# Two low-part products of 64 rows, each on its half of the array, in an fp32r SwiGLU kernel

## The chip, the cores and the metric

The kernel runs on one core of one Trainium2 chip. The metric is device time in microseconds, from runs of the whole program. Before the change the median of three runs is 514.69 us (514.53 to 514.96).

## The reference

The reference is one block of a network on 2048 tokens of 448 channels: an adaptive layer norm, a state-space convolution, a second adaptive layer norm and a SwiGLU feed-forward part with 1792 hidden units. Everything is in 32-bit floats. Cut to what matters:

```python
h = _layernorm(x, axis=-1) * (1 + ca) + sa
x = x + ga * _A_ref(h, ...)                      # the convolution
h = _layernorm(x, axis=-1) * (1 + cb) + sb
g = _silu(h @ w_gate)                            # 448 -> 1792
u = h @ w_up                                     # 448 -> 1792
x = x + gb * ((g * u) @ w_down)                  # 1792 -> 448
```

## The kernel before

The tokens are cut into 16 tiles of 128 and the tiles into six blocks of 2, 2, 3, 3, 3 and 3 tiles (`BLOCKS`). For each block `ffn` loops over the 14 slices of 128 hidden units (`f`). I call one pass of this loop a step. Each step does `gate_up(f)` and then `down(f - 1)`; between the two, and after them, small pieces of the work for the next block are put in from a table written by hand (`TIMES`, `todo`).

**Splitting into parts.** TensorE multiplies numbers of type float32r, so each operand is split into a high part (the cast to float32r) and a low part (what the cast left over). A product is the sum of high x high, low weight x high, and high weight x low. The activations lie transposed, channels on the partitions, in `hhi` and `hlo`: `[128, 4, tokens]`, four groups `k` of 128 channels. There are only 448 channels, so the fourth group has 64. These last 64 channels are laid down twice, on partitions 0 to 63 and again on 64 to 127 (`make_xn`, L162, writes channels 384 to 447 a second time).

**The weights.** `wgu[j]` is `[128, 2, 7, 128]` for slice `j`: index 0 of the second axis is gate, 1 is up. Slots 0 to 2 are the high parts of the first three groups, slots 3 to 5 their low parts. Slot 6 holds the last 64 channels in both parts: the high part on partitions 0 to 63, the low part on 64 to 127. One product of slot 6 with `hhi` thus gives high x high and low weight x high at once. `split_w` (L84 to L95) makes these parts: ScalarE casts into slots 0 to 2 and into all of slot 6, VectorE subtracts into slots 3 to 5 (L93) and into the lower half of slot 6 (L95). It runs in the prologue for slices 0 and 1 and in block 0 for the others, two steps ahead of their use.

**The products of a step.** `gate_up` takes two PSUM banks, `ps[0]` for gate and `ps[1]` for up. For each, `mm(s, False)` multiplies by `hhi`: seven products (two for each of three groups, one for slot 6). `mm(s, True)` multiplies by `hlo`: four products (slots 0, 1, 2 and 6). So there are 11 products for gate and 11 for up, 22 in a step, all of 128 rows and 128 columns of weights, with 384 columns of activations (256 in the blocks of two tiles). The order is gate high, gate low, up high, up low. In the very first step (`head`) it is gate high, up high, gate low, up low.

**After them.** ScalarE takes Silu of gate's bank (L657), VectorE multiplies it with up's bank (L662), ScalarE casts the result to its high part (L665) and VectorE makes its low part (L666). `down(f - 1)` (L677) then multiplies the previous step's result by the down weights, three products of 448 columns for each tile, into the banks `dn`, which collect over all steps. At the end of a block the next block's activations are transposed on TensorE (L169) and split.

**The prologue.** Before the first block TensorE computes modulation rows and the state of the convolution. Some of these products use weights with few columns: L186 with one column, L212 (`mod_col`) with 128 columns and then twice 64, L419 with 33. L389 are full products just ahead of L186. L231 are products that only keep TensorE running.

The queues of each engine run in the order in which the program issues the instructions. No DMA and no GpSimd work is touched by the change.

Of the kernel before, what the change touches and what calls it, by code (L numbers as in the profile page):

```python
# [12 lines left out]
OP = mybir.AluOpType  # L13
# [25 lines left out]
def f32(ap):  # L39
    return ap.bitcast(F32)  # L40
# [3 lines left out]
def tile_kernel(ctx, tc, x, a_re, a_im, b_re, b_im, c_re, c_im, log_dt, dskip,  # L44
                wg, wu, wd, c, w_mod, dft, idft, out):
    nc = tc.nc
    sy, ve, sc, po, pe = nc.sync, nc.vector, nc.scalar, nc.gpsimd, nc.tensor
# [7 lines left out]
    def bank():  # L55
        t = psg.tile([128, 512], F32, name="bank")
        return t
# [5 lines left out]
    def load_x(i):  # L63
        if i < NT:
            xs[i] = xbuf[i % len(xbuf)]
            sy.dma_start(xs[i], x[i * 128:(i + 1) * 128, :])
# [19 lines left out]
    def split_w(j, part=None):  # L86
        hi, lo, st = wgu[j][:, :, 0:3, :], wgu[j][:, :, 3:6, :], wgu[j][:, :, 6, :]
        w = raw[j]
        if not part:
            sc.copy(hi, w[:, :, 0:3, :])  # L90
            sc.copy(st, w[:, :, 3, :])
        if part is None or part == 1:
            ve.tensor_tensor(lo, w[:, :, 0:3, :], f32(hi), op=OP.subtract)  # L93
        if part is None or part == 2:
            ve.tensor_tensor(st[64:128], w[64:128, :, 3, :], f32(st[64:128]), op=OP.subtract)  # L95

    ident = const.tile([128, 128], F32)
    tri = const.tile([128, 128], F32R)
# [8 lines left out]
    hlo = const.tile([128, 4, MB * 128], F32R)  # L107
# [50 lines left out]
    def make_xn(i, new, src=None):  # L158
        src = xs[i] if src is None else src
        xn[i] = new()  # L160
        for o, a, n in ((0, 0, D), (D, 384, 64)):
            ve.tensor_scalar(xn[i][:, o:o + n], src[:, a:a + n], *n2.of[i], op0=OP.subtract, op1=OP.mult)  # L162
# [74 lines left out]
    with tc.tile_pool(name="pre", bufs=1) as pre, tc.tile_pool(name="wm", bufs=6) as wm:  # L237
# [146 lines left out]
        for q in range(2):  # L384
            ve.tensor_tensor(v1[q], h01[q], gm1, op=OP.mult)
        mm = [(0, ident, hd[0]), (0, tri, vh[0]), (1, all1, vh[0]), (1, ident, hd[1]), (1, tri, vh[1]), (1, tri, vl[1]),
              (0, tri, vl[0]), (1, all1, vl[0]), (0, ramp, v1[0]), (1, far, v1[0]), (1, ramp, v1[1])]
        for z, (q, u, v) in enumerate(mm):
            pe.matmul(os[q], u, v, start=False, stop=z in (8, 10))  # L389
        split_w(0, 0)  # L390
        scaled(wms[3], (0, 1, 2, 3))
        sb_ = added(wms[3])
# [20 lines left out]
        for z in (1, 2):  # L413
            split_w(0, z)
        transposes(TILES[0])
        o = psd.tile([128, 512], F32, name="cv")[:, 0:D]
        mm = [(left[:, 0], v) for v in vh + vl] + [(left[:, 1 + q], v1[q]) for q in range(2)]
# [200 lines left out]
    def run_blocks(pools, st, first=None):  # L618
        work, hid = pools.work, pools.hid
        new_xn = lambda: work.tile([128, 512], F32, name="xn", bufs=MB)  # L620
        def ffn(ts, fresh, last, todo):
            n = len(ts) * 128
            dn = [psd.tile([128, 512], F32, name=f"dn{q}") for q in range(len(ts))]
            pp, wp = {}, {}
            qz = [(q, z) for z in range(3) for q in range(len(ts))]

            def split_d(j):
                if last:
                    po.tensor_tensor(wdn[j], wdn[j], gb, op=OP.mult)
                hi = hid.tile([128, D], F32R, name="wdh")  # L630
                lo = hid.tile([128, D], F32R, name="wdl")
                sc.copy(hi, wdn[j])  # L632
                po.tensor_tensor(lo, wdn[j], f32(hi), op=OP.subtract)  # L633
                wp[j] = hi, lo

            def gate_up(f, nw):
                head = fresh and f == 0
                if not head:
                    split_d(f)
                w = wgu[f]  # L640
                p = hid.tile([128, MB * 128], F32, name="p")
                hi = hid.tile([128, MB * 128], F32R, name="phi")
                lo = hid.tile([128, MB * 128], F32R, name="plo")
                ps = [psd.tile([128, 512], F32, name="dn2") if head else bank(), bank()]

                def mm(s, lo):

                    parts = ((0,), (1,), (2,), (6,)) if lo else ((0, 3), (1, 4), (2, 5), (6,))
                    for k, ws in enumerate(parts):
                        for a in ws:  # L650
                            pe.matmul(ps[s][:, 0:n], w[:, s, a], (hlo if lo else hhi)[:, k, 0:n],  # L651
                                      start=not lo and a == 0, stop=lo and k == 3)

                for s, z in ((0, False), (1, False), (0, True), (1, True)) if head else (
                        (0, False), (0, True), (1, False), (1, True)):
                    mm(s, z)
                sc.activation(p[:, 0:n], ps[0][:, 0:n], AF.Silu)  # L657
                if head:
                    split_d(f)
                elif nw is not None:  # L660
                    split_w(nw, 0)
                ve.tensor_tensor(ps[1][:, 0:n], p[:, 0:n], ps[1][:, 0:n], op=OP.mult)  # L662
                if nw is not None and not head:
                    split_w(nw, 1)
                sc.copy(hi[:, 0:n], ps[1][:, 0:n])  # L665
                ve.tensor_tensor(lo[:, 0:n], ps[1][:, 0:n], f32(hi[:, 0:n]), op=OP.subtract)  # L666
                if nw is not None:
                    split_w(nw, None if head else 2)
                pp[f] = hi, lo

            def down(f, qz):
                hi, lo = pp[f]
                wh, wl = wp[f]
                for q, z in qz:
                    cs = slice(q * 128, (q + 1) * 128)
                    u, v = ((hi, wh), (hi, wl), (lo, wh))[z]
                    pe.matmul(dn[q][:, 0:D], u[:, cs], v, start=f == 0 and z == 0, stop=f == NF - 1 and z == 2)  # L677

            for f in range(NF):
                more = fresh and f + 2 < NF  # L680
                gate_up(f, f + 2 if more else None)
                if more:
                    pools.load(f + 2 + NS)
                for g, a in todo.get((f, 0), []):
                    g(*a)
                if f and not (last and f == NF - 1):
                    down(f - 1, qz)
                for g, a in todo.get((f, 1), []):
                    g(*a)
            if last:  # L690
                down(NF - 2, qz[:-1])
                down(NF - 1, [(0, 0), (0, 1)])
                down(NF - 2, qz[-1:])
                down(NF - 1, [(0, 2)] + [(q, z) for q in range(1, len(ts)) for z in range(3)])
            else:
                down(NF - 1, qz)
            for q, i in enumerate(ts):
                t = dn[q][:, 0:D]
                if not last:
                    t = new_xn()[:, 0:D]  # L700
                    ve.tensor_tensor(t, dn[q][:, 0:D], gb, op=OP.mult)
                ve.tensor_tensor(xs[i], xs[i], t, op=OP.add)
                sy.dma_start(out[i * 128:(i + 1) * 128, :], xs[i])

        for j in range(NP0, NS + 2):
            pools.load(j)
        if first is not None:
            for i in TILES[1]:
                load_x(i)
            for i in TILES[0]:  # L710
                first(i)
                n2.stat(i, TILES[0])
            n2.root(TILES[0])
            for i in TILES[0]:
                make_xn(i, new_xn)
            transposes(TILES[0])
        for b, ts in enumerate(TILES):
            todo = {}
            if b + 1 < len(TILES):
                nx = TILES[b + 1]  # L720

                def at(f, late, g, *a):
                    todo.setdefault((f, late), []).append((g, a))

                if b:
                    for i in nx:
                        at(0, 1, load_x, i)
                root1, *times, root2, shift = TIMES[min(b, 2)]

                def go(h, g, *a):  # L730
                    at(h // 2, h % 2, g, *a)

                for q, (i, hs) in enumerate(zip(nx, times)):
                    at(1 if b else q, 1, n1.stat, i, nx)
                    for h, g in zip(hs, st):
                        go(h, g, i)
                    go(h, n2.stat, i, nx)
                go(root1, n1.root, nx)
                go(root2, n2.root, nx)
                for h, i in zip(shift, nx):  # L740
                    go(h, make_xn, i, new_xn)
                at(NF - 1, 0, transposes, nx)
                if b == 0:
                    at(2, 1, end_gate)
            ffn(ts, b == 0, b + 1 == len(TILES), todo)
# [137 lines left out]
```

## Time and profile before

| | us |
|---|---|
| median of three runs | 514.69 |
| the profiled execution | 511.07 |
| its span, first to last instruction | 509.3 |
| TensorE products busy | 484.7 |
| TensorE weight loads busy | 453.9 |
| VectorE busy | 290.7 |
| GpSimd busy | 225.2 |
| ScalarE busy | 187.5 |

A row of a timeline gives the start, the length, the engine, the line of the kernel, the operation, what is written and read, the shapes and the count. PE is TensorE's products and PEld its loads of weights. For a product, `128*33` is rows x columns of the weights and `128x448` is partitions x columns of the moving operand. Products overlap: each is shown from its start to its modelled end, after the next one has begun, so the time that a product takes in a stream is read from the distance of the starts and not from the length. A row of the windows gives a stretch, its length, and then the busy time of each engine asked for with the number of instructions, and at the end the granted clock of TensorE, the share of the DMA engines and GB/s.

### The profile page before, as it was taken

Reading aid. Unit: us, or ns where it says so; the run is one execution under the profiler, and the core shown is the slowest. Engines: PE = TensorE matmul, PEld = TensorE weight load, DVE = VectorE, ACT = ScalarE, POOL = GpSimd, SP = SyncE. Lnnn points to the kernel's source line nnn. Section 1 sums busy time; section 2 is a strip of 40 time slices with the busy share of each in tenths; the row PEclk is TensorE's granted clock in tenths of the full one; section 3 lists DMA queues with packets and bytes.
Section 4 is the critical chain, followed back from the end, with each engine's and each line's share of the span. In section 5 each row is a group of like instructions: output and inputs, shape, how many; then the busy total and the mean of one; then the engine's idle time right before and its main releaser. Section 6 shows DMA issues by size and latency. Waiting matters only on the chain.

```text
span 509.3 us, 7301 instructions
## 1 busy us (share of the span) xinstructions
PE 484.7 (95%) x2747; PEld 453.9 (89%) x2747; DVE 290.7 (57%) x509; ACT 187.5 (37%) x388; POOL 225.2 (44%) x209
## 2 busy tenths in 40 slices
PE   7959988989999999999999999999999999999995
PEld 5536978879989999999899999989999989999995
DVE  2798899985786834763563575274366457211222
ACT  4347753743334422332422333243233234222221
POOL 1577474443785235553114474112556223344330
PEclk9958999999999999999999999999999999999999
DMA  7985555502000100000030000002000001000001
GB/s 220 298 204 164 169 159 145 145 1 91 1 1 2 61 31 1 0 2 0 1 108 1 2 0 2 0 36 74 1 0 2 0 1 55 0 1 1 1 0 62
DMA packets 25860, 26.07 MB, mean 51 GB/s; under 512 B 2232, under 2 KB 25144, under 8 KB 25816
## 3 DMA queue, kind: packets, MB, share of 16 engines
q1 hardware_dynamic: 25816, 25.52, 17.0%
q8 instruction: 23, 0.38, 0.3%
q14 instruction: 21, 0.17, 0.1%
HBM read 21.80 MB, written 3.67 MB: 50 GB/s over the span
## 4 chain that ended last, share of the span: by engine, by line
PE 79%; DVE 10%; issue 3%; ACT 2%; SPq 2%; DMA 2%; POOL 1%; DVEq 0%; ACTq 0%; POOLq 0%
PE bank L651 48%; PE dn L677 24%; DVE xn L162 2%; PE bank L186 2%; PE dn L389 1%; DMA dsk<-in_A_Dskip_dram 1%; DVE scr L333 1%; DVE plo L666 1%; DVE h L151 1%; PE bank L169 1%; PE bank L219 1%; DVE bank L662 1%; ACT phi L665 1%; SPq L84 1%; DMA raw<-in_B_w_up_dram 1%
## 5 line engine op out<-in xcount | busy, mean ns | idle before, releaser
L651 PE MATMUL bank<-hhi,gu 128*128 128x384 f32 (+1 forms) x1169 | 211.3, 320 | 0.0
L651 PEld LDWEIGHTS bank<-hhi,gu 128*128 128x128 f32 x1169 | 191.2, 188 | 2.7 <-issue 0.4
L633 POOL TENSOR_TENSOR wdl<-wd,wdh 128x448 fp32r<-128x448 f32 x84 | 102.2, 1218 | 201.2 <-ACT wdh L632 193.3
L651 PE MATMUL bank<-hlo,gu 128*128 128x384 f32 (+1 forms) x668 | 131.9, 319 | 0.0
L662 DVE TENSOR_TENSOR bank<-p,bank 128x384 f32<-128x384 f32 (+1 forms) x84 | 43.2, 514 | 140.0 <-PE bank L651 136.1
L651 PEld LDWEIGHTS bank<-hlo,gu 128*128 128x128 f32 x668 | 110.2, 188 | 0.0
L665 ACT CAST phi<-bank 128x384 fp32r<-128x384 f32 (+1 forms) x84 | 37.3, 444 | 147.7 <-DVE bank L662 147.7
L657 ACT ACTIVATE p<-bank 128x384 f32<-128x384 f32 (+1 forms) x83 | 37.9, 457 | 75.4 <-PE bank L651 75.3
L666 DVE TENSOR_TENSOR plo<-bank,phi 128x384 fp32r<-128x384 f32 (+1 forms) x84 | 43.0, 511 | 38.1 <-ACT phi L665 38.0
L677 PE MATMUL dn<-wdh,phi 128*128 128x448 f32 x224 | 60.1, 368 | 2.1 <-ACT phi L665 2.1
L677 PE MATMUL dn<-wdl,phi 128*128 128x448 f32 x224 | 59.6, 366 | 0.9 <-POOL wdl L633 0.9
L677 PE MATMUL dn<-wdh,plo 128*128 128x448 f32 x224 | 59.7, 367 | 0.6 <-DVE plo L666 0.6
L632 ACT CAST wdh<-wd 128x448 fp32r<-128x448 f32 x84 | 47.8, 569 | 33.3 <-PE dn L677 33.1
L677 PEld LDWEIGHTS dn<-wdl,phi 128*128 128x128 f32 x224 | 42.0, 188 | 4.7 <-POOL wdl L633 1.3
L677 PEld LDWEIGHTS dn<-wdh,plo 128*128 128x128 f32 x224 | 41.9, 188 | 4.6 <-DVE plo L666 1.2
L677 PEld LDWEIGHTS dn<-wdh,phi 128*128 128x128 f32 x224 | 39.7, 188 | 4.0 <-ACT phi L665 2.7
L762 POOL TENSOR_TENSOR v<-h,gm 128x448 f32<-128x448 f32 x14 | 16.1, 1153 | 14.0 <-DVE h L153 14.0
L769 POOL TENSOR_TENSOR v<-v,run 1x448 fp32r<-1x448 f32 x14 | 17.5, 1251 | 1.9 <-DMA run<-run 1.0
L778 POOL TENSOR_TENSOR h<-h,gd 128x448 f32<-128x448 f32 x14 | 17.6, 1258 | 0.0
L763 POOL TENSOR_TENSOR v<-h,g 128x448 fp32r<-128x448 f32 x14 | 17.6, 1254 | 0.0
L93 DVE TENSOR_TENSOR gu<-raw,gu 128x768 fp32r<-128x768 f32 x14 | 16.9, 1207 | 1.0 <-ACT gu L90 0.9
L772 ACT CAST vh<-v 128x448 fp32r<-128x448 f32 x14 | 7.9, 566 | 24.8 <-DVE v L768 24.8
(164 smaller groups left out, 434.3 us busy)
## 6 DMA issues: line engine op xcount, KB each, us to landing
wmt<-in_w_mod_dram SPq DMA_DIRECT2D x6, 784.0 KB
x<-in_A_u_dram SPq DMA_DIRECT2D x16, 224.0 KB
out_dram<-x SPq DMA_DIRECT2D x16, 224.0 KB
wd<-in_B_w_down_dram SPq DMA_DIRECT2D x14, 224.0 KB
raw<-in_B_w_gate_dram SPq DMA_DIRECT2D x14, 192.0 KB
raw<-in_B_w_up_dram SPq DMA_DIRECT2D x14, 192.0 KB
raw<-in_B_w_gate_dram SPq DMA_DIRECT2D x14, 64.0 KB
raw<-in_B_w_up_dram SPq DMA_DIRECT2D x14, 64.0 KB
```

The lines of the kernel that those rows point to most:

```text
L93: ve.tensor_tensor(lo, w[:, :, 0:3, :], f32(hi), op=OP.subtract)
L632: sc.copy(hi, wdn[j])
L633: po.tensor_tensor(lo, wdn[j], f32(hi), op=OP.subtract)
L651: pe.matmul(ps[s][:, 0:n], w[:, s, a], (hlo if lo else hhi)[:, k, 0:n], start=not lo and a == 0, stop=lo and k == 3)
L657: sc.activation(p[:, 0:n], ps[0][:, 0:n], AF.Silu)
L662: ve.tensor_tensor(ps[1][:, 0:n], p[:, 0:n], ps[1][:, 0:n], op=OP.mult)
L665: sc.copy(hi[:, 0:n], ps[1][:, 0:n])
L666: ve.tensor_tensor(lo[:, 0:n], ps[1][:, 0:n], f32(hi[:, 0:n]), op=OP.subtract)
L677: pe.matmul(dn[q][:, 0:D], u[:, cs], v, start=f == 0 and z == 0, stop=f == NF - 1 and z == 2)
L763: po.tensor_tensor(v1, h, gm1, op=OP.mult)
L769: po.tensor_tensor(v1[0:1], f32(v1[0:1]), run[0:1, 1, :], op=OP.add)
L778: po.tensor_tensor(h, h, gd, op=OP.mult)
```

## The change

The products of slot 6 with `hlo` change. Before, each was a product of 128 rows, in which the lower 64 rows multiplied the low weight with the low activation. After, each is a product of the 64 rows that hold the high weight. To let gate and up use different rows, up's slot 6 is laid out the other way round: its high part on partitions 64 to 127 and its low part on 0 to 63. The products of slot 6 with `hhi` are as before, since `hhi` holds the last 64 channels in both halves.

`split_w` makes the low part of slot 6 with two subtractions, each on 64 partitions and 128 columns, in place of one on 64 partitions and 256 columns.

In `gate_up`, `mm(s, True)` has three products, and a new function `both` issues the two products of 64 rows, one behind the other: gate's on rows 0 to 63 into `ps[0]`, up's on rows 64 to 127 into `ps[1]`. In all steps but the first, `both` stands between gate and up: its first product ends gate's sum, its second begins up's, and up's seven high products and three low ones follow. In the first step it stands between gate's low products and up's. A step still has 22 products.

The product of low weight with low activation of the last 64 channels, which the products of 128 rows had in addition, is no longer computed; for the other channels it never was.

```diff
         if part is None or part == 2:
-            ve.tensor_tensor(st[64:128], w[64:128, :, 3, :], f32(st[64:128]), op=OP.subtract)
+            for s, e in enumerate((slice(64, 128), slice(0, 64))):
+                ve.tensor_tensor(st[e, s], w[e, s, 3, :], f32(st[e, s]), op=OP.subtract)
...
                 def mm(s, lo):
-
-                    parts = ((0,), (1,), (2,), (6,)) if lo else ((0, 3), (1, 4), (2, 5), (6,))
+                    parts = ((0,), (1,), (2,)) if lo else ((0, 3), (1, 4), (2, 5), (6,))
                     for k, ws in enumerate(parts):
                         for a in ws:
                             pe.matmul(ps[s][:, 0:n], w[:, s, a], (hlo if lo else hhi)[:, k, 0:n],
-                                      start=not lo and a == 0, stop=lo and k == 3)
-
-                for s, z in ((0, False), (1, False), (0, True), (1, True)) if head else (
-                        (0, False), (0, True), (1, False), (1, True)):
-                    mm(s, z)
+                                      start=(s == 0 or head) and not lo and a == 0, stop=s == 1 and lo and k == 2)
+
+                def both(first):
+                    for s, e in enumerate((slice(0, 64), slice(64, 128))):
+                        pe.matmul(ps[s][:, 0:n], w[e, s, 6], hlo[e, 3, 0:n], start=s == 1 and first, stop=s == 0)
+
+                if head:
+                    mm(0, False)
+                    mm(1, False)
+                    mm(0, True)
+                    both(False)
+                    mm(1, True)
+                else:
+                    mm(0, False)
+                    mm(0, True)
+                    both(True)
+                    mm(1, False)
+                    mm(1, True)
```

## The prediction

> **What bounds the kernel now.** I read the page first: the busy shares, the granted clock, then the chain that ended last.
>
> ```profile
> span 509.3 us, 7301 instructions
> PE 484.7 (95%) x2747; PEld 453.9 (89%) x2747; DVE 290.7 (57%) x509; ACT 187.5 (37%) x388; POOL 225.2 (44%) x209
> PEclk9958999999999999999999999999999999999999
> PE 79%; DVE 10%; issue 3%; ACT 2%; SPq 2%; DMA 2%; POOL 1%; DVEq 0%; ACTq 0%; POOLq 0%
> ```
>
> TensorE is busy 95% of the span, at the full clock from about 50 us on, and 79% of the chain is its own work. So what the change does to TensorE's stream is what it does to the end, except where TensorE waits for others. The list of TensorE's waits, for the whole span and then for the first block alone, shows where that is:
>
> ```profile
> PE bank L219 <- DVE m L367: 6.1, 1, 6.1
> PE bank L169 <- DVE plo L666: 3.7, 5, 0.8
> PE cv L784 <- ACT vh L772: 2.1, 2, 1.5
> ```
>
> ```profile
> PE dn L677 <- ACT phi L665: 2.1, 2, 1.3
> PE cv L784 <- ACT vh L772: 1.5, 1, 1.5
> PE dn L677 <- POOL wdl L633: 0.9, 1, 0.9
> ```
>
> ```profile
> 48.00:113.00 65.00, 58.88 (x410) 54.58 (x409) 57.37 (x91) 37.63 (x83) 34.16 (x28) 1.00 0.44 126
> 113.00:172.00 59.00, 57.81 (x414) 54.97 (x413) 42.68 (x79) 23.51 (x53) 33.01 (x30) 1.00 0.07 20
> ```
>
> The last two rows give busy time per stretch (TensorE, weight loads, VectorE, ScalarE, GpSimd). The first block (48 to 113 us) needs 65 us with TensorE busy 58.88 and VectorE 57.37: there TensorE also waits for other engines. In the second block, with the same products, TensorE is busy 57.81 of 59. From there on only the handover between blocks (L169, 0.8 us each) is a wait. So a gain or loss per step counts in full in blocks 1 to 5, and only in part in block 0.
>
> **The product that is saved.** Three rows for a step with three tiles (384 columns), then for one with two (256), then the counts:
>
> ```profile
> 256.07 1.40 PE L651 MATMUL bank<-hhi,gu 128*128 128x384 f32 x7
> 258.00 1.40 PE L651 MATMUL bank<-hhi,gu 128*128 128x384 f32 x7
> 259.94 1.39 PE L651 MATMUL bank<-hhi,gu 128*128 128x384 f32 x7
> ```
>
> ```profile
> 161.05 0.99 PE L651 MATMUL bank<-hhi,gu 128*128 128x256 f32 x7
> 162.35 0.99 PE L651 MATMUL bank<-hhi,gu 128*128 128x256 f32 x7
> ```
>
> ```profile
> L651 PE MATMUL bank<-hlo,gu 128*128 128x384 f32 x448 | 96.8, 338 | 0.0
> L651 PE MATMUL bank<-hlo,gu 128*128 128x256 f32 x220 | 35.1, 281 | 0.0
> ```
>
> Gate begins at 256.07, up at 258.00, and the next unit at 259.94: eleven products every 1.93 us, 0.176 us each. (The mean of 338 ns overlaps the next product, so I use the spacing.) With two tiles it is 1.30/11 = 0.118 us. Eight low-part products per step make 448/8 = 56 steps with three tiles, and 220/8, with a few records missing, 28 with two: 14 in block 1 and 14 in block 0. Each step now has two low-part products of slot 6. Afterwards these are two products of 64 rows, with as many columns each. If both run at once they take the time of one, and a step saves 0.176 or 0.118 us. If one follows the other, it saves nothing, since the count stays 22.
>
> **What the halves cost.** No product of before uses half of the rows. The nearest rows are in the prologue, where a product uses part of the columns. First, the loads of weights as the stream goes from 128 columns to one (L389 to L186), with the products:
>
> ```profile
> 38.82 0.36 PE L389 MATMUL dn<-v,far 128*128 128x448 f32 x1
> 38.82 0.19 PEld L389 LDWEIGHTS dn<-v,ramp 128*128 128x128 f32 x1
> 39.02 0.36 PE L389 MATMUL dn<-v,ramp 128*128 128x448 f32 x1
> 39.31 0.09 PEld L186 LDWEIGHTS bank<-wmt,cs 112*1 112x1 f32 x2 [0.30 <-issue]
> 39.31 0.54 PE L186 MATMUL bank<-wmt,cs 112*1 112x448 f32 x1
> ```
>
> Inside a stream the weights of the next product are loaded as the present one starts (both at 38.82) and the products follow at 0.20. At the change of width the load begins only at 39.31, 0.29 after the last product's start, beside its product. The row names no releaser for it ("issue"), so I read it as the array emptying before the load may begin. That is 0.09 us for the wait. Here the load is of one column. What a load of 128 columns costs when nothing covers it shows where the stream starts again after an idle time:
>
> ```profile
> 105.13 0.68 PE L677 MATMUL dn<-wdl,phi 128*128 128x448 f32 x2 [0.92 <-POOL wdl L633]
> 105.64 0.57 PE L677 MATMUL dn<-wdh,plo 128*128 128x448 f32 x2
> 106.05 0.52 PE L651 MATMUL bank<-hhi,gu 128*128 128x256 f32 x3
> ```
>
> Two products take 0.51 at the restart and 0.41 after it: 0.10 us for the uncovered load. So a switch costs between 0.09 (load still covered) and 0.19 us. The second place is L212, where 128 columns become two groups of 64 and then 128 again:
>
> ```profile
> 42.44 0.74 PEld L212 LDWEIGHTS bank<-ones,wmt 112*128 112x128 f32 x6
> 43.20 0.20 PEld L212 LDWEIGHTS bank<-ones,wmt 112*64 112x64 f32 x4
> 43.41 0.18 PEld L212 LDWEIGHTS bank<-ones,row 1*128 1x128 f32 x1
> ```
>
> ```profile
> L212 PEld LDWEIGHTS bank<-ones,wmt 112*128 112x128 f32 x6 | 0.7, 190 | 0.0
> L212 PEld LDWEIGHTS bank<-ones,wmt 112*64 112x64 f32 x4 | 0.2, 134 | 0.0
> ```
>
> Six full loads of 190 ns in 0.74 us start (0.74 - 0.19)/5 = 0.11 apart, so the sixth starts at about 42.99; the next would be due at 43.10 and starts at 43.20, 0.10 late. Four half loads of 134 ns fit in 0.20, so they go two by two: independent parts of the array do work at the same time. That speaks for the pair, and the same rows speak for a wait at each change of shape. In the changed stream each step has two such changes: full to half before the pair, half to full after it.
>
> The Trainium skill, page TensorEngine Tiling (Array Packing), section Tiling Modes, states under its key properties that changing the tiling mode, and not just the tile within a mode, drains TensorE. The trace agrees for a change in columns (0.29 against 0.20); no run here shows a change in rows alone. By that rule the sum is the one that follows.
>
> I take 0.19 per switch, since both rows show the load beginning after the wait and not under it. A step with three tiles changes by 2 x 0.19 - 0.176 = +0.20 us, one with two by 2 x 0.19 - 0.118 = +0.26. Blocks 2 to 5: 56 x 0.20 = +11.2. Block 1: 14 x 0.26 = +3.6. Block 0 has the same 3.6, some of it in time in which TensorE waits anyway.
>
> **VectorE.** The split of slot 6 becomes two operations of 64 x 128 in place of one of 64 x 256, 14 times, all but the first ones in block 0.
>
> ```profile
> L666 DVE TENSOR_TENSOR plo<-bank,phi 128x384 fp32r<-128x384 f32 x56 | 31.2, 557 | 30.6 <-ACT phi L665 30.6
> L666 DVE TENSOR_TENSOR plo<-bank,phi 128x256 fp32r<-128x256 f32 x28 | 11.8, 420 | 7.6 <-ACT phi L665 7.5
> ```
>
> 128 columns more cost 137 ns, so an operation of 256 columns has 420 - 274 = 146 ns that do not depend on width, and the second operation adds about that: 14 x 0.15 = 2.1 us of VectorE. Bounds: 0 if it falls in idle time, 2.1 if all is on the path. For block 0 I take half of 3.6 + 2.1, that is +2.9 (bounds 0 and 5.7).
>
> **Waits.** Silu (L657) now waits for gate's half product. Behind the array's wait stand the other half, ten products of up, and the nine of the down stage; Silu has ten products of up (1.76 us) to finish in, so its cover holds. Up's bank is written one product earlier; the list of waits has no wait for a bank, so this is priced at nothing; without that cover it costs at most one product, 0.18, a step. No DMA is moved.
>
> **Sum.** 11.2 + 3.6 + 2.9 = +17.7 us. The profiled execution took 511.07 us (its span of 509.3 and 1.8 around it), and would take 528.8. The median of the runs is 514.69, 0.7% above; the terms are added to it alike: 532.4 us.
>
> **Rivals.** (1) Rows are not columns: no wait at a change of rows, and the halves overlap. For it: the half loads at L212 that run two by two. Against it: at L186 and L212 the load comes late. One place shows nothing late, the products of 33 columns at L419 (rows of products, then the granted clock in that stretch):
>
> ```profile
> 46.45 0.95 PE L419 MATMUL cv<-vl,left 128*33 128x448 f32 x2
> 47.20 0.95 PE L419 MATMUL cv<-v,left 128*33 128x448 f32 x2
> 47.95 1.15 PE L651 MATMUL dn<-hhi,gu 128*128 128x256 f32 x7
> ```
>
> ```profile
> 47.20:47.90 0.70, 0.70 (x3) 0.50 0.50 157
> ```
>
> The step back to 128 columns at 47.95 comes 0.75 after the last two began, as those did after the two before them, at half the clock. But 33 columns are no half or quarter of 128, so the array may well be used whole there, and I give it little weight. A second half that starts 0.01 behind (an estimate: the resolution of the rows at L212) leaves 0.166 saved per step of three tiles and 0.108 of two: 56 x 0.166 + 14 x 0.108 = 10.8, and block 0 between -1.5 and +2.1, taken as 0: 503.9 us. It decides as soon as a switch costs under 0.166/2 = 0.083 us. The Trainium skill, page TensorE: Matmul & The Clock Gate, Part 3, section on the mechanism, gives a pack of tiles the span of one product plus about 4 ns for each further tile, with nothing for entering and leaving. By that alone this rival would be the result; the loads at L212 agree on the overlap, not on the entry.
>
> (2) The array empties but the loads stay covered: 0.09 per switch. A step of three tiles changes by 0.18 - 0.17 = +0.01, one of two by +0.07; 0.6 + 1.0 and half of (1.0 + 2.1) give +3.1: 517.8 us.
>
> (3) The change doesn't do what it says: the halves follow one another, without any wait. Then only the VectorE term is left, 0 to 2.1 us, taken low: about 515.2 us.
>
> **Chances.** Forecast 0.65, with its own range 526 to 536: up by the rest of block 0 (2.9) and 0.01 of lag per step, down by block 0 at 0 and a wait that is half as long for half of the array when it is left (70 x 0.045 = 3.2). Rival 1 has 0.20, rival 2 0.10, rival 3 0.05. About 0.2% (1.0 us) is what a measurement of this kernel can tell from no change. Faster 0.20, same 0.05 (rival 3), slower 0.75. The range leaves out rival 1, two in ten, and runs from 514.5 to 536.
>
> **What would show it.** In the profile after: the load of the first half starts about 0.27 us after the start of the last full low-part product of gate (the 0.18 of its spacing and 0.09), not beside it; the two halves start within 0.02 us of each other; the load for up's first product comes some 0.3 us after the halves are issued; a step from gate to gate (with the down products) grows by 0.20 us. Weight loads' busy time falls against the span, and TensorE stays at 0.98 or more of its clock. I am wrong if the half loads start beside the last full product: then rival 1 holds if the halves start together, rival 3 if they start 0.17 apart. If the loads are early and only the products are late, it is rival 2.

## The result and the profile after

The changed kernel takes 530.59 us (median of 4 runs, 529.7 to 531.84), the kernel before 514.61 (4 runs, 512.37 to 514.96). The ratio is 1.0322, with a 95% interval of 1.0284 to 1.036: slower by 16.0 us. The profiled execution took 531.21 us (before: 511.07), its span 529.1.

First the page of the changed kernel: span, busy times, the granted clock in 40 slices, and the chain that ended last by engine.

```profile
span 529.1 us, 7315 instructions
PE 502.8 (95%) x2747; PEld 441.6 (83%) x2747; DVE 295.5 (56%) x523; ACT 188.0 (36%) x388; POOL 223.6 (42%) x209
PEclk8998989999999999999999999999999999999999
PE 72%; DVE 9%; issue 2%; DMA 2%; ACT 2%; SPq 1%; POOL 1%; ACTq 0%; DVEq 0%; POOLq 0%
```

TensorE's products fill the same 95% of a span that is 19.8 us longer, at the same clock from block 1 on (1.00; in block 0 it is 0.97, before 1.00). As many products as before (x2747) are busy 18.1 us longer. The loads of weights are busy 12.3 us less; about 10 of it is that the two loads of a pair run side by side (the page has 15.7 us for their 167 loads, and the 167 full loads of `hlo` that they replace were busy 110.2 - 84.6 = 25.6). The groups of the page say where the loads stand still (after the bar: busy us and mean ns, then the idle time of the engine just before them and what ended it). First two groups of before, then those of after:

```profile
L651 PEld LDWEIGHTS bank<-hhi,gu 128*128 128x128 f32 x1169 | 191.2, 188 | 2.7 <-issue 0.4
L95 DVE TENSOR_TENSOR gu<-raw,gu 64x256 fp32r<-64x256 f32 x14 | 10.4, 740 | 0.4
```

```profile
L653 PEld LDWEIGHTS bank<-hhi,gu 128*128 128x128 f32 x1169 | 188.4, 189 | 16.6 <-issue 10.7
L658 PEld LDWEIGHTS bank<-hlo,gu 64*128 64x128 f32 x167 | 15.7, 183 | 17.8 <-issue 13.8
L96 DVE TENSOR_TENSOR gu<-raw,gu 64x128 fp32r<-64x128 f32 x28 | 18.1, 645 | 0.9
```

Loads of weights idle 17.8 us before the halves, and 16.6 us before the `hhi` products (2.7 in the kernel before). Most of both (13.8 and 10.7) is put down to "issue", that is, no other engine is named. L653 are the full products of the changed kernel, L658 the pair, L96 the two subtractions on VectorE, treated below. (The line numbers shift a little from kernel to kernel.)

Now one passage from full products to halves and back, in the timeline of a step with 384 columns, products first and then the loads of the same time:

```profile
271.04 0.69 PE L653 MATMUL bank<-hlo,gu 128*128 128x384 f32 x3
271.66 0.44 PE L658 MATMUL bank<-hlo,gu 64*128 64x384 f32 x2
272.03 1.50 PE L653 MATMUL bank<-hhi,gu 128*128 128x384 f32 x7
273.37 0.69 PE L653 MATMUL bank<-hlo,gu 128*128 128x384 f32 x3
```

```profile
270.86 0.55 PEld L653 LDWEIGHTS bank<-hlo,gu 128*128 128x128 f32 x3
271.66 0.18 PEld L658 LDWEIGHTS bank<-hlo,gu 64*128 64x128 f32 x2 [0.25 <-issue]
272.03 1.19 PEld L653 LDWEIGHTS bank<-hhi,gu 128*128 128x128 f32 x7 [0.19 <-issue]
```

In the stream the load for a product starts about one product ahead of it: 270.86 for 271.04. At both changes this lead is gone. Of gate's three low products the last starts at 271.04 + 2 x 0.176 = 271.39. The loads of the halves begin only at 271.66, 0.27 later, together with their products; up's first load begins at 272.03, 0.37 after the halves. Then seven products of up take 273.37 - 272.03 = 1.34, where seven in the stream take 1.23: the first one also waits 0.11 for its load. Over the passage, 0.27 + 0.37 + 0.29 (up's first product) = 0.93 stand in place of four products of 0.176, 0.70. That is 0.22 us more per step.

The two loads take 0.18 together, at a mean of 183 ns each (L658 above), and the two products 0.44 with 438 ns each in the group of 384 columns: the halves do run side by side. The Trainium skill, page TensorEngine Tiling (Array Packing), section Tiling Modes, says that a change of mode drains TensorE and that tiles work independently. These rows agree with both, for rows now, with 0.25 and 0.19 us of idle loads at the two changes.

The length of a step, from gate's first product to the next one's, in block 5 of before and of after:

```profile
484.90 1.40 PE L651 MATMUL bank<-hhi,gu 128*128 128x384 f32 x7
...
490.60 1.40 PE L651 MATMUL bank<-hhi,gu 128*128 128x384 f32 x7
```

```profile
485.42 1.40 PE L653 MATMUL bank<-hhi,gu 128*128 128x384 f32 x7
...
491.35 1.40 PE L653 MATMUL bank<-hhi,gu 128*128 128x384 f32 x7
```

5.70 has become 5.93. By blocks, in the windows (the stretch, its length, then busy time of TensorE, weight loads, VectorE, ScalarE and GpSimd, the granted clock, DMA share and GB/s), before and after:

```profile
47.95:112.98 65.03, 58.91 (x409) 54.62 (x408) 57.39 (x91) 37.68 (x83) 34.21 (x28) 1.00 0.44 126
112.98:172.13 59.15, 57.96 (x414) 55.10 (x413) 42.83 (x79) 23.64 (x54) 33.01 (x30) 1.00 0.06 20
172.13:256.07 83.94, 83.11 (x456) 80.80 (x455) 45.44 (x83) 28.11 (x56) 33.99 (x31) 1.00 0.05 15
```

```profile
48.70:116.97 68.27, 63.53 (x409) 56.14 (x408) 61.07 (x108) 37.62 (x83) 33.64 (x28) 0.97 0.43 127
116.97:178.68 61.71, 61.21 (x415) 55.42 (x414) 42.67 (x79) 23.83 (x54) 32.98 (x30) 1.00 0.06 20
178.68:265.73 87.05, 86.22 (x457) 77.85 (x455) 45.24 (x83) 28.15 (x55) 33.98 (x31) 1.00 0.04 14
```

The three rows of each are blocks 0, 1 and 2. Block 2 takes 87.05 in place of 83.94: 3.1 us for 14 steps, 0.22 each, and block 3, with 87.07, does the same. Block 1 takes 61.71 in place of 59.15.

### The profile page after: what moved, and what is told of

The parts are those of the page before. It is cut to its first block, busy times and chain, and to the rows that moved or that the text cites. A ratio compares the mean times of both kernels' runs of the same rounds, so it can differ in the third digit from the quotient of the medians.

```text
span 529.1 us, 7315 instructions
## 1 busy us (share of the span) xinstructions
PE 502.8 (95%) x2747; PEld 441.6 (83%) x2747; DVE 295.5 (56%) x523; ACT 188.0 (36%) x388; POOL 223.6 (42%) x209
## 4 chain that ended last, share of the span: by engine, by line
PE 72%; DVE 9%; issue 2%; DMA 2%; ACT 2%; SPq 1%; POOL 1%; ACTq 0%; DVEq 0%; POOLq 0%
PE bank L653 43%; PE dn L692 22%; PE bank L658 5%; DVE gu L96 1%; DVE gu L93 1%; DVE xn L163 1%; DMA raw<-in_B_w_up_dram 1%; DVE plo L681 1%; DMA wd<-in_B_w_down_dram 1%; DVE bank L677 1%; DVE v L783 1%; ACT phi L680 1%; SPq L78 1%; PE bank L170 0%; POOL wdl L634 0%
## 5 line engine op out<-in xcount | busy, mean ns | idle before, releaser
L653 PE MATMUL bank<-hhi,gu 128*128 128x384 f32 (+1 forms) x1169 | 221.1, 328 | 0.0
L653 PEld LDWEIGHTS bank<-hhi,gu 128*128 128x128 f32 x1169 | 188.4, 189 | 16.6 <-issue 10.7
L653 PE MATMUL bank<-hlo,gu 128*128 128x384 f32 (+1 forms) x501 | 106.3, 320 | 0.0
L653 PEld LDWEIGHTS bank<-hlo,gu 128*128 128x128 f32 x501 | 84.6, 189 | 0.1
L658 PE MATMUL bank<-hlo,gu 64*128 64x384 f32 (+1 forms) x167 | 35.6, 421 | 0.0
L658 PEld LDWEIGHTS bank<-hlo,gu 64*128 64x128 f32 x167 | 15.7, 183 | 17.8 <-issue 13.8
L187 PE MATMUL bank<-wmt,cs 112*128 112x448 f32 (+1 forms) x32 | 15.4, 632 | 4.7 <-DMA wmt<-in_w_mod_dram 4.7
L96 DVE TENSOR_TENSOR gu<-raw,gu 64x128 fp32r<-64x128 f32 x28 | 18.1, 645 | 0.9
L784 POOL TENSOR_TENSOR v<-v,run 1x448 fp32r<-1x448 f32 x14 | 17.5, 1247 | 1.8 <-DMA run<-run 1.0
```

The costliest lines, as they stand in the source:

```text
L96: ve.tensor_tensor(st[e, s], w[e, s, 3, :], f32(st[e, s]), op=OP.subtract)
L658: pe.matmul(ps[s][:, 0:n], w[e, s, 6], hlo[e, 3, 0:n], start=s == 1 and first, stop=s == 0)
L784: po.tensor_tensor(v1[0:1], f32(v1[0:1]), run[0:1, 1, :], op=OP.add)
```

## The experiments

The theory, as it stood ahead of these runs: TensorE empties before it loads weights for another array shape, and that load is uncovered; each change costs about 0.2 us, whatever runs between, and the halves are otherwise as fast as was hoped. The rivals: the price belongs to products with fewer than 128 rows as such; or to the second half (the halves get in each other's way); or to the VectorE edit. The first four kernels share runs of the kernel before with a median of 513.91 us (19 runs), the last three with 513.81 (18 runs).

**Fewer rows, same shape (x1_rows65).** On the kernel before:

```diff
-                            pe.matmul(ps[s][:, 0:n], w[:, s, a], (hlo if lo else hhi)[:, k, 0:n],
+                            r = slice(0, 65 if lo and k == 3 else 128)
+                            pe.matmul(ps[s][:, 0:n], w[r, s, a], (hlo if lo else hhi)[r, k, 0:n],
```

> The kernel before, with the low-part products of slot 6 on rows 0 to 64 (65 rows) for gate and for up; left out is the product of the low weight with the low activation for 63 of the last 64 channels. Theory (the cost is that the array changes its shape): 65 rows are no half, the array keeps its shape, and the time is that of before, 514.6 us within 1. Rival (products with fewer than 128 rows are slow in themselves, or the saved half of the rows matters): 520 us or more, or a gain.

515.03 us against 513.91, ratio 1.0011 (0.9986 to 1.0036): no difference. The group of its products, and a step in block 5:

```profile
L652 PE MATMUL bank<-hlo,gu 65*128 65x384 f32 x112 | 38.2, 341 | 0.0
```

```profile
496.11 1.39 PE L652 MATMUL bank<-hhi,gu 128*128 128x384 f32 x7
...
501.84 1.39 PE L652 MATMUL bank<-hhi,gu 128*128 128x384 f32 x7
```

A product of 65 rows lasts 341 ns where the full one lasts 338, and the step 5.73. A product that leaves 63 rows empty costs nothing that the times can tell (and saves nothing). The price is not in having fewer rows.

**One half only (x2_one_half).** On the changed kernel; up's product of slot 6 is a full one again, at the end of up, and gate's half stands alone between full products:

```diff
-                    parts = ((0,), (1,), (2,)) if lo else ((0, 3), (1, 4), (2, 5), (6,))
+                    parts = ((0,), (1,), (2,)) + ((6,),) * s if lo else ((0, 3), (1, 4), (2, 5), (6,))
...
-                    for s, e in enumerate((slice(0, 64), slice(64, 128))):
-                        pe.matmul(ps[s][:, 0:n], w[e, s, 6], hlo[e, 3, 0:n], start=s == 1 and first, stop=s == 0)
+                    pe.matmul(ps[0][:, 0:n], w[0:64, 0, 6], hlo[0:64, 3, 0:n], start=False, stop=True)
```

> The changed kernel, but only gate's low-part product of slot 6 is of 64 rows; up's is a full product again, in its old place at the end of up. So a step has two changes of shape and saves nothing. Theory (two changes of shape per step, the second half free): the changed kernel plus one product per step, 56 x 0.176 + 14 x 0.118 + up to 1.7 in block 0 = 11.5 to 13, so 542 to 544 us. Rival (the cost comes from the two halves getting in each other's way, at their banks or in the array): one half alone is harmless, 515 to 518 us.

541.88 us, 0.1 under the theory's range, ratio 1.0554 (1.0509 to 1.0598). The same passage:

```profile
271.75 0.44 PE L657 MATMUL bank<-hlo,gu 64*128 64x384 f32 x1
272.13 1.49 PE L653 MATMUL bank<-hhi,gu 128*128 128x384 f32 x7
```

One half keeps TensorE from 271.75 to 272.13, 0.38, and lasts 0.44; the two halves of the changed kernel took 0.37 and 0.44. So the second half is free. With nothing saved, a step (gate's first products at 280.23 and 286.32 in the same timeline) takes 6.09 in place of 5.70: the two changes cost 0.39. The rival of the halves that hinder each other is out.

**The pair twice (x3_pair_twice).** Each pair is issued twice:

```diff
-                    for s, e in enumerate((slice(0, 64), slice(64, 128))):
-                        pe.matmul(ps[s][:, 0:n], w[e, s, 6], hlo[e, 3, 0:n], start=s == 1 and first, stop=s == 0)
+                    for z in range(2):
+                        for s, e in enumerate((slice(0, 64), slice(64, 128))):
+                            pe.matmul(ps[s][:, 0:n], w[e, s, 6], hlo[e, 3, 0:n],
+                                      start=s == 1 and first and z == 0, stop=s == 0 and z == 1)
```

> The changed kernel with the pair of halves issued twice in a row (the low activation's term of the last 64 channels counts twice). Theory (the price is per change of shape, and inside the shape the halves run together at the rate of one product): one product time more per step, 542 to 544 us. Rival A (each pair pays its own wait and load): 0.37 us per step more, 558 us or above. Rival B (the halves only start together and then run one after the other): two product times more, 553 to 556 us.

541.92 us, 0.1 under the theory's range and far from both rivals, ratio 1.0538 (1.0498 to 1.0578).

```profile
503.32 0.62 PE L659 MATMUL bank<-hlo,gu 64*128 64x384 f32 x4
503.87 1.50 PE L653 MATMUL bank<-hhi,gu 128*128 128x384 f32 x7
```

From the halves to up it is now 0.55, 0.18 more than with one pair. A further pair inside the shape costs what one full product costs; only going in and coming out costs extra.

**The subtraction alone (x4_two_splits).** The kernel before, with L95 as two operations:

```diff
-            ve.tensor_tensor(st[64:128], w[64:128, :, 3, :], f32(st[64:128]), op=OP.subtract)
+            for s in range(2):
+                ve.tensor_tensor(st[64:128, s], w[64:128, s, 3, :], f32(st[64:128, s]), op=OP.subtract)
```

> The kernel before with the subtraction of slot 6 as two operations of 64 x 128, layout and products as before. Theory (the VectorE term is small): 514.6 to 516.7 us, most likely 515.6. Rival (a good part of the 16 us comes from VectorE in block 0): 518 us or more.

516.32 us, ratio 1.005 (1.0026 to 1.0073): +2.4 us, between 1.3 and 3.8. The time lies in the theory's range; the difference is a little above the +2.1 at which that range ends, since before's median is lower in these runs. So the edit on VectorE has a cost clear of noise, and it is a small part of the 16.

**Fewer columns (x5_columns).** On the kernel before:

```diff
-                    for k, ws in enumerate(parts):
-                        for a in ws:
-                            pe.matmul(ps[s][:, 0:n], w[:, s, a], (hlo if lo else hhi)[:, k, 0:n],
-                                      start=not lo and a == 0, stop=lo and k == 3)
+                    for k in (3, 0, 1, 2) if lo else range(4):
+                        for a in parts[k]:
+                            c = slice(0, 64 if lo and k == 3 and s == 0 else 128)
+                            pe.matmul(ps[s][c, 0:n], w[:, s, a, c], (hlo if lo else hhi)[:, k, 0:n],
+                                      start=not lo and a == 0, stop=lo and k == 2)
```

> The kernel before, with gate's low-part product of slot 6 cut to 64 columns of weights (and issued first of gate's four low-part products); what it leaves out is the other 64 output rows of that product. All other products are full, so each step has two changes of array shape, in columns and not in rows, and no product is saved. Theory (a change of shape in columns costs what one in rows costs, about 0.40 us for going in and coming out with 384 columns and 0.38 with 256): 56 x 0.40 + 28 x 0.38 = +33, less what block 0 and other stalls absorb, as in the run with one half of the rows: 541 to 545 us. Rival A (the price belongs to halves of the rows only, columns are free): 513 to 516 us. Rival B (columns cost half as much, about 0.2 for the two changes): 526 to 531 us.

514.03 us against 513.81, ratio 1.0 (0.9978 to 1.0021). Here the theory as I had put it missed by 27 us. The time is that of rival A, no change was paid for, but the run doesn't show that a change in columns is free:

```profile
493.34 0.87 PE L652 MATMUL bank<-hlo,gu 128*64 128x384 f32 x4
494.04 1.40 PE L652 MATMUL bank<-hhi,gu 128*128 128x384 f32 x7
```

```profile
493.16 0.72 PEld L652 LDWEIGHTS bank<-hlo,gu 128*64 128x64 f32 x4
493.87 1.24 PEld L652 LDWEIGHTS bank<-hhi,gu 128*128 128x128 f32 x7
```

The group takes its name from its first product, the one with 64 columns. Four products in 0.70 and the loads 0.18 and 0.17 ahead: the plain stream. What failed was my premise that 64 columns are another shape. In the compiled program each product's instruction names the groups of the array's rows and columns that it goes to. These products still name all four groups of columns, as those of the 33 columns at L419 do, which showed no late load either; those of L186 name one group and those of L212 two, and there the load was late. With rows it is the same: the products of 65 rows name all four groups of rows, the halves of the changed kernel two. So in these runs it is not the number of columns or rows that decides, but whether the product is addressed to a part of the array. What a change in columns costs in the main loop was not measured.

**Fewer visits (x6_every_second, x7_every_fourth).** On the changed kernel, with `times` pairs in a step. Every fourth:

```diff
+                times = (2 if f == 1 else 4) * (f % 4 == 1)
...
-                    for s, e in enumerate((slice(0, 64), slice(64, 128))):
-                        pe.matmul(ps[s][:, 0:n], w[e, s, 6], hlo[e, 3, 0:n], start=s == 1 and first, stop=s == 0)
+                    for z in range(times):
+                        for s, e in enumerate((slice(0, 64), slice(64, 128))):
+                            pe.matmul(ps[s][:, 0:n], w[e, s, 6], hlo[e, 3, 0:n],
+                                      start=s == 1 and first and z == 0, stop=s == 0 and z == times - 1)
```

Every second has `times = 2 * (f % 2)`. In steps without a pair the full products begin and end the sums (an edit of `start` and `stop` that is left out above).

> The changed kernel, with no pair of halves in every other step and the pair issued twice in the others: as many pairs and as many full products as the changed kernel, but 42 visits to the shape of 64 rows in place of 84. It leaves out the slot-6 low part of every other step and adds that of the others twice. Theory (the price is per visit): a visit costs 0.22 + 0.176 = 0.40 us with 384 columns, 0.26 + 0.118 = 0.38 with 256, and each pair then saves one product of 0.176 or 0.118: 28 x (0.40 - 0.352) + 14 x (0.38 - 0.236) = +3.3, and +2.5 of VectorE for the second subtraction: 518 to 521 us where the kernel before takes 514. Rival (the price is per half product, whatever stands beside it): as the changed kernel, 529 to 532 us.

> The changed kernel with four visits a block (24 in all) to the shape of 64 rows, each with the pairs of two to four steps, 84 pairs in all as in the changed kernel. It leaves out the slot-6 low part of the steps without a visit and adds that of the others two or four times. Theory (per visit): 16 x 0.40 - 56 x 0.176 = -3.5, 8 x 0.38 - 28 x 0.118 = -0.3, and +2.5 of VectorE: -1.3, that is 511 to 514 us where the kernel before takes 514. Rival (per half product): 529 to 532 us. If VectorE's second subtraction costs nothing here, 510 to 511.

Every second step: 518.73 us, ratio 1.011 (1.0061 to 1.0159). Every fourth: 511.93 us, ratio 0.9965 (0.9943 to 0.9987). Both lie in the theory's ranges, and far from 529 to 532; every fourth is 1.9 us faster than before, clear of noise but small. The steps of block 5, first with every second, then with every fourth:

```profile
462.76 1.40 PE L653 MATMUL bank<-hhi,gu 128*128 128x384 f32 x7
...
468.11 1.39 PE L653 MATMUL bank<-hhi,gu 128*128 128x384 f32 x7
469.96 0.62 PE L661 MATMUL bank<-hlo,gu 64*128 64x384 f32 x4
...
474.21 1.04 PE L653 MATMUL bank<-hhi,gu 128*128 128x384 f32 x5
```

```profile
468.74 1.39 PE L653 MATMUL bank<-hhi,gu 128*128 128x384 f32 x7
...
474.08 1.40 PE L653 MATMUL bank<-hhi,gu 128*128 128x384 f32 x7
475.94 0.97 PE L661 MATMUL bank<-hlo,gu 64*128 64x384 f32 x8
476.84 1.50 PE L653 MATMUL bank<-hhi,gu 128*128 128x384 f32 x7
```

A step without slot 6 takes 5.35 in the one and 5.34 in the other, two products less than 5.70. The step with two pairs takes 6.10, so two steps take 11.45 where the kernel before takes 11.40: no gain. Four pairs take 0.90 from the first half to up (475.94 to 476.84), 0.37 + 3 x 0.18. So four steps take 0.3 less than the 22.80 of before (3 x 5.34 and 6.47 for the one with the pairs), and block 3 takes 83.14 us in place of 84.01.

By these figures pairs pay from three in a visit on (three were not run). With the slot-6 part of every step kept, four pairs in one visit need the sums of four steps, eight PSUM banks, open at once; the kernel has four for gate and up beside three for `dn` and one for the convolution. Two pairs would fit, and are worth nothing. A stream that stays in the shape of 64 rows through the whole loop was not tried.

## Why the prediction was right, and where its terms were off

**The bound.** Right: TensorE's stream sets the end, and blocks 1 to 5 carry the difference. From the start of block 1 to the end of the span it is 529.1 - 116.97 = 412.1 after, and 509.3 - 112.98 = 396.3 before: +15.8 of the 16.0 between the medians. Of this +15.0 lies in the steps, and +0.8 behind TensorE's last product (6.5 us to the end of the span, 5.7 before). `x4_two_splits`, where the products are those of before, has 6.6 there, so that part is not the price of a change of shape; what makes it is not shown.

**The price of a change.** Right in mechanism and nearly in size. Predicted 0.19 for each; measured (0.23 + 0.176)/2 = 0.20 with 384 columns. The rows fit the parts of the prediction: 0.27 to the halves' loads is 0.176 and 0.09 before the load, as forecast; 0.37 to up's load (I had said "some 0.3") can be split into an uncovered load of 0.10, the product's 0.176 and 0.09 again; the last 0.11 is the uncovered load of up's first product. That the 0.09 is the array emptying is my reading: the rows show that the load starts late and that no other engine is named for it. Steps of three tiles grew by 0.23 where 0.20 was forecast, blocks 2 to 5 by 4 x 3.1 = 12.4 where 11.2 was.

**The saving.** Right: the halves run together and take the time of one. `x2_one_half` and `x3_pair_twice` show it, so rivals 1 and 2 fail on the price alone. Rival 1 needed a switch below 0.083 us. Rival 2 needed covered loads; the loads are as late as the products. Rival 3 (halves in turn) is excluded by the row of 0.44 us for two.

**Block 1.** +2.6 where I had +3.6. A step of two tiles grew by 0.26 as forecast, but one wait went. In before's timeline the convolution's product waited for ScalarE:

```profile
143.96 0.47 PE L784 MATMUL cv<-vh,tri 128*128 128x448 f32 x1 [0.60 <-ACT vh L772]
```

In the changed kernel the same place has no wait: TensorE comes there later, and the other engines have time to finish. Most of the rest lies at the next products of the convolution and at the handover to block 2, which are 0.1 and 0.2 us shorter. A loss on TensorE's path is smaller where it stood waiting, which I had allowed for in block 0 only; yet the two lists of waits that the prediction shows already had 2.1 us at L784 in all and 1.5 in block 0, which leaves these 0.6 behind it.

**Block 0.** I forecast +2.9, half of what a full price gives. The profiles read alone show 65.03 to 68.27, +3.2; but that is no confirmation. In the kernel with 65 rows, equal to before in the medians, block 0 takes 68.50 (first row; 67.93 in `x5_columns`), and in `x2_one_half`, where each step pays for the changes and saves nothing, 68.39 (second row):

```profile
49.08:117.58 68.50, 61.23 (x409) 56.37 (x408) 58.26 (x94) 37.72 (x83) 33.59 (x28) 0.97 0.46 131
49.08:117.47 68.39, 64.79 (x410) 57.59 (x408) 60.84 (x107) 37.64 (x83) 33.69 (x28) 0.97 0.44 125
```

The clock there is 0.97 in both, as in the changed kernel, and 1.00 in before's profile, which was an execution 3.5 us below its median. At one clock, then, block 0 is as long with the price as without it. TensorE is busy longer and waits less: its waits on other engines in block 0 add up to 7.3 us in `x1_rows65`, 4.8 in the changed kernel and 3.6 in `x2_one_half`. So the 1.8 that I took for the pair in block 0 (half of 3.6) was too large; in these profiles nothing of it is seen, within the half microsecond or so by which these lengths differ. The medians agree: what is left for everything ahead of block 1 is 16.0 - 15.8 = 0.2 us, with an uncertainty of 2 us from the interval of the ratio.

`x4_two_splits` had +2.4 for the subtraction. In its profile 0.9 of that lies behind TensorE's last product (6.6 us against 5.7), where no subtraction is done, and block 0 takes 69.32 at a clock of 0.98, 0.8 more than with 65 rows. That is about what I took for the subtraction in block 0 (half of 2.1), but 1.2 us of uncertainty and single profiles don't tell it closely.

**VectorE.** I took 0.146 us for what a second operation adds. Undisturbed that is right: in the trace an operation on 128 columns takes 0.282 us at the least and one on 256 takes 0.422, so two add 0.14. But the means are 645 ns, against 740 ns for one of 256 in before: 2 x 645 - 740 = 550 ns a step, four times the estimate. The reason is in the last section.

**Waits.** Right: in the list after, TensorE waits neither for Silu nor for a bank that was not yet free. Its entries are those of before and of the prologue.

**The sum.** +17.7 forecast, +16.0 measured: blocks 2 to 5 are 1.2 more, block 1 is 1.0 less, block 0 about 2.7 less, and some 0.8 us more lies behind the last step. Errors both ways cancel in part, so the sum is nearer than its terms; that part is luck. The sum was made on before's profile and its terms added to the median as they stand; since block 0 differs between executions, that carried the term of block 0 over unchecked.

## What to carry to other kernels

A product on half of the array's rows takes no longer than a full one, and two on different halves run as one; what costs is each change between full and half, here 0.2 us, in which the load of weights loses its lead over the products and starts some 0.09 us late. Where TensorE waits for other engines anyway, as in block 0, the price vanishes in the wait. Count the products saved per visit: with 0.176 us a product, more than 0.40/0.176 = 2.3 must be saved each time the stream leaves the full shape. To see whether a narrow product is such a change, look for a load of weights that starts with its product and not ahead of it.

## What the runs showed of the hardware that was not expected

**Two subtractions, and GpSimd between.** A VectorE operation with both inputs in SBUF may wait for one of GpSimd to end. In the changed kernel, VectorE first, then GpSimd:

```profile
55.07 1.46 DVE L96 TENSOR_TENSOR gu<-raw,gu 64x128 fp32r<-64x128 f32 x2
```

```profile
54.89 1.17 POOL L634 TENSOR_TENSOR wdl<-wd,wdh 128x448 fp32r<-128x448 f32 x1 [1.16 <-ACT wdh L633]
```

The two subtractions should take 2 x 0.28. GpSimd's ends at 54.89 + 1.17 = 56.06; VectorE's first one, begun at 55.07, ends 0.15 after that, at 56.21, and its second then takes 0.28, with the pair over at 56.53. It is no single case. Of the 28 subtractions in this trace 14 take 0.28 to 0.29 us and 14 take 0.61 to 1.22; of these, 12 end 0.14 or 0.15 us after a GpSimd operation that was under way when they began. So each operation is one more chance to fall behind GpSimd's, and a short one may take over a microsecond. The Trainium skill, page SBUF — State Buffer, section "SBUF: two separate sides", says that a VectorE operation with two SBUF inputs and a GpSimd operation that reads SBUF exclude each other for the whole instruction; these rows agree.

**A narrow product need not be a change of shape.** 65 rows or 64 columns of weights (`x1_rows65`, `x5_columns`) changed the time by 0.1% and 0.0%, within their intervals, in a step of 22 products with two and one such products; the same data addressed to half of the array's rows cost 0.4 us a step.
